# First batch: 1/Z folded into the summing matrix, the first tile divided at its store

## The chip, the cores and the metric

The kernel runs on one core of a Trainium2 chip. Its engines are TensorE (PE; its weight loads are listed apart as PEld), VectorE (DVE), ScalarE (ACT), GpSimd (POOL) and SyncE (SP, which issues the transfers); each works through its own queue in order, and they wait for one another by semaphores. The metric is the device time of one execution in microseconds. Before the change it is 1436.37 us, the median of 3 runs (1436.26 to 1436.56).

## The reference, cut to what matters

`x` is 4 x 12480 x 128, `inducing` 32 x 128, the feed-forward weights are 128 x 2048 and 2048 x 128. Inputs are float32 or, for the weights, doubles that the kernel turns into float32.

```python
def mab(q, kv):
    s = scale * (q @ kv.transpose(0, 2, 1))
    s = s - s.max(-1, keepdims=True)
    a = np.exp(s)
    a /= a.sum(-1, keepdims=True) + 1e-09
    return a @ kv
h = mab(I, x)                 # 32 inducing rows over 12480 rows, for each of 4 batches
x = mab(x, h)                 # each row over the 32 rows of h
h = x @ w_in
g = np.maximum(0.01 * h, h)
out = g @ w_out
```

## The kernel before, in words

**Tiles.** Each batch of 12480 rows is cut in six groups of 2048 rows and a rest of 192. A *tile* is 512 rows; tile 0 and tile 1 are the first two of batch 0. For a tile the kernel never forms `mab(x, h)`: with A the transposed softmax weights of its 512 rows (32 x 512, written four times, one copy for each 32 partitions), the first layer is `(h @ w_in)^T`-weights times A. The first-layer weights in that form are `hwhi` and `hwlo`, a high and a low part, made from h by `weights_product` and `split_weights`. A has a high and a low part too, and each first-layer block `f` (16 of 128 columns) is three products: hi·hi, lo·hi and hi·lo (`first_products`, line L1171). Four blocks are worked on side by side, each on 32 of the array's rows. The result goes through a ReLU on ScalarE (`ghi`, L1140) and leaves a low part (`glo`) that VectorE (L1144) or GpSimd (L1114 and L1116) makes; the second layer is three products again with `w_hi` and `w_lo` (L1202, a *triple* below). The linear part of the leaky ReLU goes by `w12` = 0.01·w_in·w_out (`setup_w12`, L349 to L357; `linear_part`, L1214).

**The start.** `first_batch` streams batch 0 in, and for each group forms scores against the inducing rows, a running maximum and sum, exponentials, and the weighted sum of rows `hacc`. When the last group is in, `sums` gives 1/Z as a column `rz`, `normalise` scales `hacc` by it on ScalarE (L674) and multiplies with the constant matrix `e128`, whose columns sum over the four positions at which a row of h lies (L680); a copy gives `hT` (L684). Beside it run: the conversion of the weights from doubles (`from_double`: `cv_a` on ScalarE, `cv_b`, `cv_a` and `cv_t` on VectorE, the last sum on GpSimd), the turning of w_in (`turn_w_in`, L318, copied at L324 or L326), the split of w_out (`split_w_out`, `w_hi` on ScalarE, `w_lo` on GpSimd), and `keep_going` (L337), products that nobody reads.

**The first two tiles.** Tiles 0 and 1 take a short way, `quick`: scores of the tile's 512 rows straight against `hT` (four products, L1029), maximum and subtraction on VectorE (L1036, L1040), exponential on ScalarE (L1044), sum, +1e-9, reciprocal and scaling on VectorE (L1047 to L1050), then 16 products with the identity that turn the weights and write them four times (L1058), and the copy into A, high part on ScalarE (L1064), low part on VectorE (L1067). Every other tile takes `second`, `softmax` and `stack`, the same in parts that run beside the feed-forward.

**The order.** All of it is emitted under a manual schedule: what stands later in a queue stays later. In the start the order is written by hand: `ROUNDS` and `DRAIN` say which side lane (`t` turning, `l` conversions, `s` split, `k` unread products, `d` turning with a VectorE copy) steps at which point of `first_batch`; then a tuple of lanes (L1312) orders the two `quick`s and the making of the first-layer weights; then the loop over `rounds` emits first-layer blocks of tiles 0 and 1 in turns of four, and after each second-layer triple the steps of `others(u)`, with `u` the count of triples. `first_round` emits the twelve first-layer products of four blocks. From tile 2 on a planner with modelled engine times sets the order. Eight PSUM banks are handed out in turn from small groups (`turns`); a bank is written again only when its reader is done. `store` (L1224 on) turns a finished tile on VectorE into `osb` and stores it by four transfers.

Of the kernel before, what the change touches and what calls it, by code (L numbers as in the profile page):

```python
# [19 lines left out]
def induced_attention_then_leaky_ffn(  # L20
# [24 lines left out]
    P = 128  # L45
# [33 lines left out]
    ]  # L79
    DRAIN = ["", "", "ll", "lldkk", "", ""]  # L80

# [87 lines left out]
    def new(engine, at=0.0):  # L169
        if quads[0]:  # L170
            yield engine, at
# [8 lines left out]
    def gen_ps(name):  # L180
        return bank("gen")
# [151 lines left out]

    def keep_going():
        while True:
            pt = gen_ps("keep_ps")
            nc.tensor.matmul(pt[:, : 2 * P], ident, w_in_sb[:, : 2 * P], start=True, stop=True)  # L337
            done(pt)
            yield

    def setup_w12():
        for c in range(NF // 4):
            while c >= len(ready):
                yield
            if c == len(ready) - 1:
                yield from idle(4)
# [322 lines left out]
    def normalise(b, hacc, rz):  # L669

        same = e128.rearrange("p j m -> p (j m)")
        yield from new(ACT, clock[DVE])
        hs = sb.tile([P, C], F32, tag="hs", name="hs", bufs=1)
# [18 lines left out]
    def first_batch():  # L692
# [98 lines left out]
        hacc = added(0, order[n - 2], hacc, al, hp)  # L791
        scale = sums(0)
        yield next(bg)
# [229 lines left out]
    def quick(t):  # L1023
# [13 lines left out]
        if not qys:  # L1037
            qys.append(sb.tile([P, QUICK, 4, M], F32, tag="both", name="qy", bufs=2))
        y = qys[0][:, t]
# [6 lines left out]
        sm = sb.tile([P, 4], F32, tag="sm", name="qsm")  # L1046
        nc.vector.tensor_reduce(out=sm, in_=y, op=ALU.add, axis=AX.X)  # L1047
        nc.vector.tensor_scalar_add(sm, sm, 1e-9)
        nc.vector.reciprocal(sm, sm)
        nc.vector.tensor_tensor(  # L1050
            out=y, in0=y, in1=sm.unsqueeze(2).broadcast_to([P, 4, M]), op=ALU.mult
        )
        yield
# [8 lines left out]
        yield  # L1062
        A4[t] = a4 = sb.tile([P, 2, TOK], F32R, tag="A4", name="A4", bufs=A4_BUFS)
# [7 lines left out]
        done(pa, at)  # L1071
        yield


    tiles = []
# [148 lines left out]
    def store(t, total, summed, at=0.0):  # L1224
# [9 lines left out]
        at = spent(DVE, BLOCKS, at)  # L1234
        if summed:
            parts_used[0] -= 1
        else:
            done(total, at)
# [58 lines left out]
    with tc.manual_schedule():  # L1297
        setup()
        late = [chain(setup_w_in(), setup_w_out())]
        turning, splits, twelve = [turn_w_in()], [parts_of_w_out()], [setup_w12()]  # L1300
        lanes = {"t": turning, "l": late, "s": splits, "k": [keep_going()]}
        for todo in first_batch():
# [6 lines left out]
        weights = [expand_weights(0)]  # L1309
        one, two, keep = [quick(0)], [quick(1)], lanes["k"]  # L1310
        for lane in (
            one, weights, two, one, weights, one, weights, one, keep, one, two, late, one, two,  # L1312
        ):
            step(lane)
# [5 lines left out]

        first_round(*rounds[0])
        timing[0] = True
        stacks[0] = stacks[0][QUICK:]
# [442 lines left out]
```

## Time and profile before

| | us |
|---|---|
| median of 3 runs | 1436.37 (1436.26 to 1436.56) |
| span of the profiled execution | 1434.7 |
| TensorE busy in it | 1418.0 |
| VectorE, ScalarE, GpSimd busy | 1070.6, 1066.0, 1178.9 |

The profiled execution is known by its span, from the first instruction to the last; the median of the timed runs lies 1.7 us above it. The rows below are of five kinds. The page is a summary of the whole span. The table by stretches gives the busy time of each engine between two moments, with the granted clock of TensorE as a share of its full rate. The timeline lists instructions in order of time, equal ones merged, with the idle time of the engine ahead of them in brackets and the instruction that ended it. The chain of waits is followed back from the last instruction, at each step to what released it. Times are from the start of the span. A matmul record's end is modelled and holds the array's latency, so that records overlap; the distance from one start to the next is what a product costs the queue. A float32 product that is no transpose shows as two records (passes).

### The profile page before, as it was taken

How to read it: one execution, taken by the hardware profiler on the slowest of the kernel's cores; microseconds unless marked ns; L12 is line 12 of the kernel's file. 1: busy time of each engine (PE TensorE's matmuls, PEld its weight loads, DVE VectorE, ACT ScalarE, POOL GpSimd, SP SyncE). 2: the span in 40 equal slices, each digit the busy share in tenths (PEclk: the TensorE clock that was granted, in tenths of full speed). 3: DMA queues.
4: the chain of work that ended last, by engine and by line, in shares of the span. 5: the costliest groups of instructions: out<-in, count | busy, mean ns of one | idle time of the engine just before them, and what ended most of it. 6: DMA issues, size and time to landing. Idle time of an engine off the chain costs nothing.

```text
span 1434.7 us, 60214 instructions
## 1 busy us (share of the span) xinstructions
PE 1418.0 (99%) x25207; PEld 1301.2 (91%) x25207; DVE 1070.6 (75%) x1913; ACT 1066.0 (74%) x1956; POOL 1178.9 (82%) x1237
## 2 busy tenths in 40 slices
PE   8999999999999999999999999999999999999998
PEld 6679899998889899998899999999989999999997
DVE  6777787776777787877777777877787876777664
ACT  6567777777777777777777787777777877778775
POOL 2369999899999888899999998885557588969996
PEclk9999999999999999999999999999999999999999
DMA  8055556433454553464445445534222333233231
GB/s 297 13 115 101 107 109 123 97 82 86 97 99 89 116 94 56 75 146 107 99 91 95 88 84 111 114 87 110 57 61 59 64 63 66 45 64 69 56 67 23
DMA packets 400703, 128.49 MB, mean 90 GB/s; under 512 B 373136, under 2 KB 375600, under 8 KB 400432
## 3 DMA queue, kind: packets, MB, share of 16 engines
q1 hardware_dynamic: 399328, 124.50, 41.7%
q8 instruction: 198, 3.24, 1.0%
q14 instruction: 73, 0.60, 0.1%
q10 hardware_dynamic: 1104, 0.15, 0.1%
HBM read 48.94 MB, written 25.56 MB: 52 GB/s over the span
## 4 chain that ended last, share of the span: by engine, by line
PE 94%; DVE 2%; ACT 1%; DMA 1%; issue 1%; POOL 1%; SPq 1%; DVEq 0%; ACTq 0%; POOLq 0%
PE bank L1171 87%; PE bank L398 3%; PE bank L578 2%; PE bank L1202 1%; DVE glo L1144 1%; PE bank L725 1%; DMA xr<-in_x_dram 1%; ACT ghi L1140 0%; DMA out_dram<-osb 0%; PE bank L820 0%; SPq L1012 0%; ACT xT L731 0%; POOL glo L1447 0%; PE bank L1058 0%; SPq L703 0%
## 5 line engine op out<-in xcount | busy, mean ns | idle before, releaser
L1171 PE MATMUL bank<-glo,w_hi 32*128 32x512 f32 (+1 forms) x6080 | 1165.1, 375 | 0.0
L1171 PE MATMUL bank<-ghi,w_hi 32*128 32x512 f32 (+1 forms) x6080 | 1164.7, 375 | 0.2
L1171 PE MATMUL bank<-ghi,w_lo 32*128 32x512 f32 (+1 forms) x6080 | 1164.8, 374 | 0.0
L1171 PE MATMUL bank<-A,hwhi 32*128 32x512 f32 (+1 forms) x3394 | 993.6, 373 | 0.8 <-DVE glo L1144 0.4
L1144 DVE SCALAR_TENSOR_TENSOR glo<-bank,ghi 128x512 fp32r<-128x512 f32 (+1 forms) x1047 | 687.2, 681 | 254.1 <-ACT ghi L1140 241.4
L1171 PEld LDWEIGHTS bank<-ghi,w_hi 32*128 32x128 f32 x6080 | 805.1, 184 | 16.5 <-issue 2.7
L1171 PEld LDWEIGHTS bank<-ghi,w_lo 32*128 32x128 f32 x6080 | 807.0, 184 | 12.4 <-issue 2.0
L1171 PEld LDWEIGHTS bank<-glo,w_hi 32*128 32x128 f32 x6080 | 806.8, 184 | 11.8 <-issue 1.0
L1140 ACT ACTIVATE ghi<-bank 128x512 fp32r<-128x512 f32 (+1 forms) x1047 | 608.0, 597 | 151.3 <-PE bank L1171 128.4
L1447 POOL TENSOR_TENSOR glo<-g,ghi 128x512 fp32r<-128x512 f32 (+1 forms) x513 | 656.0, 1279 | 41.1
L1171 PE MATMUL bank<-A,hwlo 32*128 32x512 f32 (+1 forms) x1697 | 586.2, 370 | 0.0
L1171 PEld LDWEIGHTS bank<-A,hwhi 32*128 32x128 f32 x3394 | 564.9, 184 | 16.6 <-DVE glo L1144 2.4
L1140 ACT ACTIVATE g<-bank 128x512 f32<-128x512 f32 (+1 forms) x521 | 311.2, 598 | 146.7 <-PE bank L1171 87.5
L1445 POOL CAST ghi<-g 128x512 fp32r<-128x512 f32 (+1 forms) x513 | 312.9, 610 | 106.5 <-ACT g L1140 80.0
L1171 PEld LDWEIGHTS bank<-A,hwlo 32*128 32x128 f32 x1697 | 299.9, 184 | 2.6 <-issue 0.2
L1481 DVE TENSOR_TENSOR part<-bank,part 128x512 f32<-128x512 f32 (+1 forms) x190 | 130.0, 685 | 60.7 <-PE bank L1171 38.3
L1492 POOL TENSOR_TENSOR part<-part 128x512 f32<-128x512 f32 (+1 forms) x95 | 121.4, 1277 | 22.5 <-DVE part L1481 22.1
L1474 ACT COPY part<-bank 128x512 f32<-128x512 f32 (+1 forms) x190 | 110.7, 584 | 12.4 <-PE bank L1171 10.5
L1229 DVE STREAM_TRANSPOSE osb<-part 128x512 f32<-128x512 f32 (+1 forms) x95 | 66.6, 701 | 6.6 <-POOL part L1492 4.9
L534 DVE STREAM_TRANSPOSE xT<-xc 128x512 f32<-128x512 f32 x72 | 46.5, 684 | 0.0
L455 ACT ACTIVATE e<-e,nm 128x512 f32<-128x512 f32 (+1 forms) x28 | 18.7, 667 | 22.9 <-DVE least L443 22.7
L936 POOL TENSOR_TENSOR y<-y,mx 128x512 f32<-128x512 f32 (+1 forms) x24 | 24.4, 1018 | 9.6 <-DVE mx L932 8.3
(135 smaller groups left out, 646.1 us busy)
## 6 DMA issues: line engine op xcount, KB each, us to landing
A<-both SPq DMA_DIRECT2D x376, 128.0 KB, 2.4
xr<-in_x_dram SPq DMA_DIRECT2D x96, 256.0 KB, 4.3
out_dram<-osb SPq DMA_DIRECT2D x382, 64.0 KB, 2.2
xc<-in_x_dram SPq DMA_DIRECT2D x288, 64.0 KB, 2.9
raw<-in_moe_w_in_dram SPq DMA_DIRECT2D x4, 512.0 KB, 6.6
raw<-in_moe_w_out_dram SPq DMA_DIRECT2D x4, 512.0 KB, 7.4
A<-both SPq DMA_DIRECT2D x48, 16.0 KB, 1.8
out_dram<-osb SPq DMA_DIRECT2D x48, 8.0 KB, 1.8
```

What stands on the lines that cost most here:

```text
L398: nc.tensor.matmul(dst, lhsT, rhs, start=True, stop=True)
L534: nc.vector.transpose(t[:, j, :], blk.rearrange("p n c -> p (n c)"))
L578: nc.tensor.matmul(hp[32 * k : 32 * k + 32, :C], ay[:rows_, 4 * q + k, :], xb[:rows_, k, :], start=(q == 0), stop=(4 * q + 4 >= K), tile_p ...
L1140: nc.scalar.activation(ghi, ph, AF.Relu)
L1144: nc.vector.scalar_tensor_tensor(out=glo, in0=ph, scalar=0.0, in1=ghi, op0=ALU.max, op1=ALU.subtract,)
L1171: nc.tensor.matmul(dst, w[32 * r : 32 * r + 32], woven(x[32 * r : 32 * r + 32]), start=start, stop=stop, tile_position=(32 * r, 0),)
L1229: nc.vector.transpose(osb[:, :n], total[:, :n])
L1445: nc.gpsimd.tensor_copy(ghi[:, :n], g[:, :n])
L1447: nc.gpsimd.tensor_tensor(out=glo[:, :n], in0=g[:, :n], in1=ghi[:, :n].bitcast(F32), op=ALU.subtract)
L1474: nc.scalar.copy(put, got)
L1481: nc.vector.tensor_tensor(out=put, in0=got, in1=put, op=ALU.add)
L1492: nc.gpsimd.tensor_tensor(out=total[:, :n], in0=total[:, :n], in1=part[:, :n], op=ALU.add)
```

## The change

Four edits, all in the start of batch 0 and in the store of tile 0.

- `first_batch` makes `scale`, the constant `e128` times `rz`, on ScalarE as soon as `rz` is there; `normalise` for batch 0 multiplies `hacc` itself with it.
- `quick(0)` doesn't divide by the sum. Its exponential is written four times (two ScalarE instructions of 128 x 256), so that four transposes of 128 x 128 give the four copies of the turned weights. The sums, their reciprocals, and 16 small products that turn the reciprocals into one factor per partition and 32 columns (`over`) come at `u == 7`. `store` multiplies `osb` of tile 0 by `over` on GpSimd. (The layers behind are homogeneous, so that a positive factor per row may come at the end.)
- `keep_going` is gone.
- The hand-written orders move: the last turning of w_in goes from the first rounds into `DRAIN` (`"t"` in place of `"kk"` and the empty steps), `late` goes ahead of `one`, the second tile's `quick` behind the first one's, and the first step of `w12` behind the first `first_round`.

The diff, cut:

```diff
-    DRAIN = ["", "", "ll", "lldkk", "", ""]
+    DRAIN = ["", "", "ll", "lld", "", "t"]
...
+        if not b:
+            ph = aux_ps("hT_ps")
+            nc.tensor.matmul(ph[:, :P], hacc, rz, start=True, stop=True)
+            yield
+            hT = sb.tile([P, P], F32, tag="hT", name="hT")
+            nc.scalar.copy(hT, ph[:, :P])
...
-        scale = sums(0)
+        rz = sums(0)
+        scale = sb.tile([P, P], F32, tag="hs", name="scale", bufs=1)
+        nc.scalar.mul(scale, e128.rearrange("p j m -> p (j m)"), rz)
...
-        nc.scalar.activation(y, y, AF.Exp, scale=SCALE)
+        if t:
+            nc.scalar.activation(y, y, AF.Exp, scale=SCALE)
+        else:
+            four = qys[0][:, : 4 * P].rearrange("p (c r m) -> p c r m", r=4, m=M)
+            for c in (0, 2):
+                nc.scalar.activation(
+                    four[:, c : c + 2], y[:, c : c + 2].unsqueeze(2).broadcast_to([P, 2, 4, M]),
+                    AF.Exp, scale=SCALE,
+                )
...
         for c in range(4):
+            if not t:
+                nc.tensor.transpose(
+                    pa[:, c * P : (c + 1) * P], qys[0][:, c * P : (c + 1) * P], ident
+                )
+                continue
             for r in range(4):
...
+        sm = total(four[:, :, 0])
+        pr = aux_ps("rows_ps")
+        rows_of_k = pr[:, : 4 * 4].rearrange("p (c a) -> p c a", a=4)
+        for a in range(4):
+            for r in range(4):
+                nc.tensor.matmul(
+                    rows_of_k[32 * r : 32 * r + 32, :, a], ident[:, 32 * a : 32 * a + 32], sm,
+                    start=True, stop=True, tile_position=(0, 32 * r),
+                )
+        over = sb.tile([P, 16], F32, tag="over", name="over", bufs=1)
+        nc.scalar.copy(over, pr[:, :16])
...
+            nc.gpsimd.tensor_tensor(
+                out=ov, in0=ov, in1=overs[t].unsqueeze(2).broadcast_to([P, 16, 32]), op=ALU.mult
+            )
...
-            one, weights, two, one, weights, one, weights, one, keep, one, two, late, one, two,
-        ):
+        for lane in (late, one, weights, one, weights, weights, one, two, one, two, two):
             step(lane)
...
         first_round(*rounds[0])
+        step(twelve)
...
+                if u == 7:
+                    step(one)
```

**Place 1.** TensorE from the third turning of w_in (L318) to the turned weights of the two quick tiles, before: L337 are the unread products, L680 the summing product, L1029 the scores, L820 the first-layer weights, L1058 the 16 products that turn tile 0's weights.

```order
L318 MATMUL bank_65<-ident,w_in_sb 128x128 x4
L337 MATMUL bank_66<-w_in_sb,ident 128x256
L337 MATMUL bank_64<-w_in_sb,ident 128x256
L680 MATMUL bank_70<-e_74,hs 128x128
L1029 MATMUL bank_71<-hT,xT 128x32 x4
L820 MATMUL bank_70<-w_in_sb,hT 32x512 x4
L1029 MATMUL bank_65<-hT,xT 128x32 x4
L1058 MATMUL bank_67<-ident,qy 32x128 x16
L337 MATMUL bank_66<-w_in_sb,ident 128x256
```

The same stretch now; L667 is the summing product, L1035 the scores, L826 the first-layer weights, L1078 the transposes.

```order
L318 MATMUL bank_65<-ident,w_in_sb 128x128 x4
L667 MATMUL bank_70<-scale,hacc 128x128
L318 MATMUL bank_66<-ident,w_in_sb 128x128 x4
L1035 MATMUL bank_71<-hT,xT 128x32 x4
L826 MATMUL bank_70<-w_in_sb,hT 32x512 x4
L1078 MATMUL bank_67<-ident,qy 128x128 x4
L1035 MATMUL bank_64<-hT,xT 128x32 x4
```

The unread products are gone, the fourth turning of w_in stands behind the summing product, and the second tile's scores stand behind the transposes of the first.

**Place 2.** TensorE in the second turn of four blocks, before: triples of tile 1 (bank3_67; here the tiles are printed with their numbers) and the next first products of tile 1 (A4_752).

```order
L1202 MATMUL bank3_67<-ghi_779,w_hi_77 128x512
L1202 MATMUL bank3_67<-ghi_779,w_lo_78 128x512
L1202 MATMUL bank3_67<-glo_780,w_hi_77 128x512
L1202 MATMUL bank3_67<-ghi_783,w_hi_77 128x512
L1202 MATMUL bank3_67<-ghi_783,w_lo_78 128x512
L1202 MATMUL bank3_67<-glo_784,w_hi_77 128x512
L1171 MATMUL bank5_69<-A4_752,hwhi_659 128x512
L1171 MATMUL bank1_65<-A4_752,hwhi_659 128x512
```

The same now; L1107 are the 16 small products, L342 a step of w12.

```order
L1247 MATMUL bank3_67<-ghi_771,w_hi_77 128x512
L1247 MATMUL bank3_67<-ghi_771,w_lo_78 128x512
L1247 MATMUL bank3_67<-glo_772,w_hi_77 128x512
L1107 MATMUL bank7_71<-qsm_837,ident_72 32x4 x16
L1247 MATMUL bank3_67<-ghi_775,w_hi_77 128x512
L1247 MATMUL bank3_67<-ghi_775,w_lo_78 128x512
L1247 MATMUL bank3_67<-glo_776,w_hi_77 128x512
L342 MATMUL bank6_70<-wraw_619,winT_569 128x128 x4
L1216 MATMUL bank1_65<-A4_744,hwhi_662 128x512
L1216 MATMUL bank2_66<-A4_744,hwhi_662 128x512
```

The small products stand between two triples, ahead of the next first products. VectorE at the same place, before: the last low part of tile 0's second four blocks, a conversion (L216), maximum and subtraction of a softmax (L932, L936), a conversion (L220), and low parts of tile 1's second four blocks.

```order
L1144 SCALAR_TENSOR_TENSOR glo_829<-bank0_64,ghi_828 128x512
L216 TENSOR_SCALAR cv_b_837<-raw_308 128x512
L932 TENSOR_REDUCE mx_846<-y_800 128x16
L936 TENSOR_TENSOR y_800<-y_800,mx_846 128x512
L220 SCALAR_TENSOR_TENSOR cv_a_836<-cv_a_836,cv_b_837 128x512
L1144 SCALAR_TENSOR_TENSOR glo_873<-bank5_69,ghi_872 128x512
L1144 SCALAR_TENSOR_TENSOR glo_883<-bank2_66,ghi_882 128x512
```

The same now; L1063 to L1065 make the sums' reciprocals, and the small products read them.

```order
L1189 SCALAR_TENSOR_TENSOR glo_815<-bank0_64,ghi_814 128x512
L216 TENSOR_SCALAR cv_b_823<-raw_308 128x512
L938 TENSOR_REDUCE mx_827<-y_786 128x16
L942 TENSOR_TENSOR y_786<-y_786,mx_827 128x512
L220 SCALAR_TENSOR_TENSOR cv_a_822<-cv_a_822,cv_b_823 128x512
L1063 TENSOR_REDUCE qsm_837<-qy_658 128x4
L1064 TENSOR_SCALAR qsm_837<-qsm_837 128x4
L1065 RECIPROCAL qsm_837<-qsm_837 128x4
L348 SCALAR_TENSOR_TENSOR w12_79<-bank6_70,w12_79 128x128
L1189 SCALAR_TENSOR_TENSOR glo_881<-bank1_65,ghi_880 128x512
```

The three short steps stand behind the conversions and the softmax's subtraction, and a step of w12 (L348) stands ahead of the low parts.

**Place 3.** GpSimd around the first store, before: w_lo's last part, a low part, a softmax's subtraction (L936) and the low part of A (L996).

```order
L288 TENSOR_TENSOR w_lo<-wraw,w_hi 128x512
L1114 CAST ghi<-g 128x512
L1116 TENSOR_TENSOR glo<-g,ghi 128x512
L936 TENSOR_TENSOR y<-y,mx 128x512
L996 TENSOR_TENSOR both<-aT,both 128x512
L1445 CAST ghi<-g 128x512
```

The same now.

```order
L288 TENSOR_TENSOR w_lo<-wraw,w_hi 128x512
L1159 CAST ghi<-g 128x512
L1161 TENSOR_TENSOR glo<-g,ghi 128x512
L1282 TENSOR_TENSOR osb<-osb,over 128x512
L942 TENSOR_TENSOR y<-y,mx 128x512
L1002 TENSOR_TENSOR both<-aT,both 128x512
L1496 CAST ghi<-g 128x512
```

The multiply of osb stands ahead of the subtraction. Behind these places the order of every engine is the same as before, in operations and tiles (bank and buffer numbers apart), to the end.

## Rows read from the trace of the kernel before

**Rows 1.** The profile's page, its first line.

```profile
span 1434.7 us, 60214 instructions
```

**Rows 2.** Busy time by stretch: us; busy us (instructions) per engine, granted clock, DMA share, GB/s.

```profile
36.00:56.00 20.00, 18.16 (x227) 11.76 (x228) 14.65 (x34) 10.41 (x22) 5.70 (x5) 1.00 0.04 7
...
56.00:64.00 8.00, 8.00 (x55) 6.45 (x54) 6.17 (x11) 5.38 (x11) 3.57 (x4) 1.00 0.00 0
...
64.00:92.00 28.00, 26.59 (x168) 17.71 (x170) 23.45 (x43) 14.05 (x27) 15.02 (x15) 1.00 0.38 70
...
160.00:1400.00 1240.00, 1238.54 (x22872) 1152.59 (x22872) 934.28 (x1617) 944.29 (x1723) 1061.31 (x1113) 1.00 0.43 87
```

**Rows 3.** Timeline, 38 to 48 us: start, duration (us), engine, line, operation, [idle before].

```profile
38.49 0.35 DVE L597 SCALAR_TENSOR_TENSOR hacc<-hacc,al,bank 128x128 f32<-128x128 f32 x1 [0.34 <-PE bank L578]
...
40.45 1.08 PE L1029 MATMUL bank<-hT,xT 128*128 128x32 f32 x8 [0.35 <-ACT hT L684]
...
44.79 0.58 ACT L1064 CAST A<-bank 128x512 fp32r<-128x512 f32 x1 [1.60 <-PE bank L1058]
...
46.67 2.07 ACT L1140 ACTIVATE ghi<-bank 128x512 fp32r<-128x512 f32 x4 [1.08 <-PE bank L1171]
...
47.30 2.48 DVE L1144 SCALAR_TENSOR_TENSOR glo<-bank,ghi 128x512 fp32r<-128x512 f32 x4
```

**Rows 4.** Timeline, 53 to 62 us, TensorE and VectorE.

```profile
53.28 0.66 PE L318 MATMUL bank<-ident,w_in_sb 128*128 128x128 f32 x4 [0.56 <-DVE glo L1144]
...
54.86 0.49 PE L1171 MATMUL bank<-A,hwhi 32*128 32x512 f32 x4
...
55.40 0.38 PE L1171 MATMUL bank<-A,hwhi 32*128 32x512 f32 x4
...
56.47 1.05 PE L349 MATMUL bank<-wraw,winT 128*128 128x128 f32 x8
...
56.93 1.89 DVE L1144 SCALAR_TENSOR_TENSOR glo<-bank,ghi 128x512 fp32r<-128x512 f32 x3 [1.21 <-ACT ghi L1140]
...
60.47 0.68 DVE L220 SCALAR_TENSOR_TENSOR cv_a<-cv_a,cv_b 128x512 int32<-128x512 int32 x1
...
61.73 0.69 DVE L1144 SCALAR_TENSOR_TENSOR glo<-bank,ghi 128x512 fp32r<-128x512 f32 x1 [0.58 <-ACT ghi L1140]
```

**Rows 5.** Timeline: small operations of the first batch.

```profile
34.24 0.39 PE L482 MATMUL bank<-rd,e 128*128 128x4 f32 x2 [0.21 <-DVE rd L424]
...
42.55 0.29 DVE L1047 TENSOR_REDUCE qsm<-qy 128x4 f32<-128x128 f32 x1 [0.38 <-ACT qy L1044]
...
48.46 1.08 PE L1058 MATMUL bank<-ident,qy 128*32 128x128 f32 x32
```

**Rows 6.** Stretches of TensorE alone: us, busy us (instructions), granted clock, DMA share, GB/s.

```profile
11.00:12.00 1.00, 0.26 (x2) 0.93 1.04 410
...
1430.00:1432.00 2.00, 0.00 (x0) 0.95 0.25 44
```

**Rows 7.** Chain of waits: start, duration (us), engine, tile, line, instructions.

```profile
11.74 3.62 PE bank L725 x16
...
17.09 1.90 PE bank L725 x16
...
91.41 27.90 PE bank L1171 x491
```

**Rows 8.** Timeline, 91 to 98 us: first store, GpSimd, ScalarE, one TensorE product.

```profile
91.47 1.43 DVE L1233 STREAM_TRANSPOSE osb<-bank 128x256 f32<-128x256 f32 x4
...
91.73 1.05 POOL L936 TENSOR_TENSOR y<-y,mx 128x512 f32<-128x512 f32 x1
...
94.89 1.28 POOL L1447 TENSOR_TENSOR glo<-g,ghi 128x512 fp32r<-128x512 f32 x1
...
96.46 0.63 ACT L1140 ACTIVATE g<-bank 128x512 f32<-128x512 f32 x1
...
97.45 0.37 PE L1171 MATMUL bank<-A,hwhi 32*128 32x512 f32 x1
```

More of the change, by code (lines that the diff above doesn't have):

```diff
@@ L332, in turn_w_in @@
             yield
[L334 to L339, printed above, removed]
     def setup_w12():
@@ L344, in setup_w12 @@
                 yield
-            if c == len(ready) - 1:
+            if c and c == len(ready) - 1:
                 yield from idle(4)
@@ L671, in normalise @@
         same = e128.rearrange("p j m -> p (j m)")
+        if not b:
[4 more added lines that the diff above has]
+            nc.scalar.copy(hT, ph[:, :P])
+            done(ph)
+            hw[b] = [hT, None, None, False]
+            finishing[0] = 1
+            yield
+            return
         yield from new(ACT, clock[DVE])
@@ L1037, in quick @@
         if not qys:
-            qys.append(sb.tile([P, QUICK, 4, M], F32, tag="both", name="qy", bufs=2))
-        y = qys[0][:, t]
+            qys.append(sb.tile([P, 4 * P + 2 * P], F32, tag="both", name="qy", bufs=2))
+        y = qys[0][:, 4 * P + t * P : 4 * P + (t + 1) * P].rearrange("p (c m) -> p c m", m=M)
         nc.vector.tensor_tensor(
@@ L1043, in quick, with total @@
         done(sp)
-        nc.scalar.activation(y, y, AF.Exp, scale=SCALE)
-        yield
[L1046 to L1053, printed above, removed]
+        if t:
[7 more added lines that the diff above has]
+                )
+        yield
+        def total(y):
+            sm = sb.tile([P, 4], F32, tag="sm", name="qsm")
+            nc.vector.tensor_reduce(out=sm, in_=y, op=ALU.add, axis=AX.X)
+            nc.vector.tensor_scalar_add(sm, sm, 1e-9)
+            nc.vector.reciprocal(sm, sm)
+            return sm
+        if t:
+            sm = total(y)
+            nc.vector.tensor_tensor(
+                out=y, in0=y, in1=sm.unsqueeze(2).broadcast_to([P, 4, M]), op=ALU.mult
+            )
+            yield
         pa = bank("out")
@@ L1061, in quick @@
                 )
-        yield
+        if t:
+            yield
         A4[t] = a4 = sb.tile([P, 2, TOK], F32R, tag="A4", name="A4", bufs=A4_BUFS)
@@ L1072, in quick @@
         yield
+        if t:
+            return
+        sm = total(four[:, :, 0])
+        spent(DVE, 640.0)
+        pr = aux_ps("rows_ps")
[8 more added lines that the diff above has]
+        nc.scalar.copy(over, pr[:, :16])
+        at = spent(ACT, 200.0, on_array("c", 60.0))
+        done(pr, at)
+        overs[t] = over
+        yield
+    overs = {}
     tiles = []
@@ L1234, in store @@
         at = spent(DVE, BLOCKS, at)
+        if t in overs:
+            ov = osb.rearrange("p (k c) -> p k c", c=32)
+            nc.gpsimd.tensor_tensor(
+                out=ov, in0=ov, in1=overs[t].unsqueeze(2).broadcast_to([P, 16, 32]), op=ALU.mult
+            )
         if summed:
@@ L1300, in induced_attention_then_leaky_ffn @@
         turning, splits, twelve = [turn_w_in()], [parts_of_w_out()], [setup_w12()]
-        lanes = {"t": turning, "l": late, "s": splits, "k": [keep_going()]}
+        lanes = {"t": turning, "l": late, "s": splits}
         for todo in first_batch():
@@ L1309, in induced_attention_then_leaky_ffn @@
         weights = [expand_weights(0)]
-        one, two, keep = [quick(0)], [quick(1)], lanes["k"]
-        for lane in (
-            one, weights, two, one, weights, one, weights, one, keep, one, two, late, one, two,
-        ):
+        one, two = [quick(0)], [quick(1)]
+        for lane in (late, one, weights, one, weights, weights, one, two, one, two, two):
             step(lane)
```

## The prediction, before the run

> **What bounds the kernel now.** I read the table by stretches first. From 160 to 1400 us TensorE is busy 1238.54 of 1240.00 us; in 64 to 92 us it is busy 26.59 of 28.00 [rows 2], and the chain of waits runs on TensorE alone for 27.90 us from 91.41 us [rows 7]. So past some 92 us the order of TensorE's work is the time: a microsecond that its queue is late there stays to the end, and one that it is early is kept. The order of the changed kernel is the same as before, engine by engine, after that point, but for one GpSimd multiply at the first store. The change is therefore decided between 38 and 92 us, and there I read the timeline row by row [rows 3, 4].
>
> In that stretch two engines take turns as the bound. Up to 47 us it is one serial chain (h, scores, softmax, A, first layer, ReLU) [rows 3]. From 57 us on VectorE has no room: the three low parts that start at 56.93, the conversions of w_out and a softmax follow each other to 61.15, then the next low part starts at 61.73 [rows 4]. What VectorE does behind that (conversions, from which GpSimd makes w_lo, for which TensorE waits) sets TensorE's pace up to 92 us. So the moment at which this row of 61.73 us starts is my measure of the whole start.
>
> **The change part by part.**
>
> *1/Z in the summing matrix, no unread products.* h's sum is ready on VectorE at 38.49 + 0.35 = 38.84; the scaling on ScalarE, the unread products, the summing product and a copy follow, and the first scores start at 40.45 [rows 3]. Now the product reads the sum itself, and the scaled matrix is made on ScalarE before the sum is there: the product goes at about 38.9, the scores at about 39.65, 0.8 earlier. The turning of the last chunk of w_in fills the wait for h; before, it stood at 53.28 [rows 4].
>
> *Undivided exponentials, written four times.* Between the exponential and the cast of A at 44.79 [rows 3] stand four VectorE steps, the first at 42.55, and 32 passes (1.08) [rows 5]. The steps go away, the passes become four transposes. It costs a second exponential and one cast ahead on ScalarE, some 0.4 and 0.5. By these steps the cast of A is at about 43.05, 1.7 earlier. But this does not carry through. The second tile's scores now come behind the transposes (until about 43.9), its maximum and subtraction behind A's low part (until about 44.9), and the fourth first-layer product writes the bank in which those scores lay; so the ReLUs go at 45.6, not at 46.67. The second tile's division still stands ahead of the first low part on VectorE: about 46.25 instead of 47.30 [rows 3]. I take **1.05 earlier**; the ends are 0.8 (nothing but the first item) and 1.7 (the cast's gain carries through).
>
> *The moved turning.* Without the turning and its wait at 53.28, the first products of blocks 4 to 7 of tile 0 are held by the low part of tile 1's fourth block alone: their third group, at 55.40 before [rows 4], starts at about 54.15, 1.25 earlier.
>
> *The four steps, put back later.* The sums of the first tile, their reciprocals and their turning (16 small products) still have to be made. In the new order VectorE has them behind the three low parts, a conversion, a maximum, a subtraction and another conversion; TensorE has the 16 products ahead of block 3 of tile 1. That is a new wait, with the whole TensorE queue behind it. TensorE is there three triples after the third group: 54.15 + 0.31 + 3 x 0.65 = 56.4. VectorE needs from that third group to the end of the second conversion what it needed before, 60.47 + 0.68 - 55.40 = 5.75 [rows 4], and then a reduction of 0.29 as in [rows 5] and two short steps, 0.7 together: 54.15 + 5.75 + 0.7 + 0.05 = 60.65. **TensorE waits 4.2 us.**
>
> Nothing covers this. Behind it TensorE has the 16 products, block 3, a w12 product and the next first products, whose ReLU and low part VectorE waits for. The trace has no product of this shape. Its bounds are 0.4 (two passes with 4 columns, 0.39, if the other 30 passes cost next to nothing) and 1.08 (32 passes with 128 columns) [rows 5]; I take 0.9, nearer to the second, which has the same number of passes and of weight loads. So the low part that was at 61.73 starts at 60.65 + 0.9 + 0.85 (block 3 and two changes of tiling) + 0.8 (the w12 product: 56.47 to its successor) + 0.92 (twelve first products, 54.86 to 55.78) + 0.65 (one ReLU and its signals) = 64.8: **3.05 later**. One w12 step of VectorE is now ahead of it, which gives back 0.2: **2.85**. What stood ahead of 61.73 before was ScalarE's exponential, so none of the start's gain is left there.
>
> *The clock.* The granted clock was at the upper level (2.4 GHz, shown as 1.00) in all of 36 to 92 us [rows 2]. It fell to the lower one in the stretch 11 to 12 us, after TensorE had been busy 0.26 us of one, and in 1430 to 1432, a stretch without a product [rows 6]. Sixteen transposes took 3.62 us there and 1.90 at the upper level: 1.7 lost [rows 7]. A wait of 4.2 us is longer than that second stretch, so I expect a fall in it. The low level begins partly inside the wait, where it costs nothing: I take **1.2**, with ends 0 (no fall) and 2.4 (a second such stretch in part).
>
> The Trainium skill speaks against the change here. "TensorE: Matmul & The Clock Gate", Part 1 (the HAM clock gate), says that "the default state is throttled, and activity releases the throttle"; the change takes out the unread products, which were activity alone, and adds a wait. By that page the clock would fall in the new wait, and the sum would be 1441.2 with it and 1440.0 without; the two falls in the trace agree.
>
> *The scaling at the store.* GpSimd gets a 128x512 multiply ahead of the subtraction that started at 91.73; it waits for the first two of the four pieces of osb, until about 92.2, and takes about 1.05, as the subtraction of that shape did [rows 8]. So GpSimd is 1.5 late, less 0.15 of idle time: 1.35. Its next low part, 94.89 + 1.28, frees the buffer (g has two) that the ScalarE row of 96.46 writes (slack 0.3), and that row frees the bank that TensorE writes at 97.45 (slack 0.35) [rows 8]. TensorE is held for about **0.75**; ends 0 and 1.35. SyncE's store waits 1.1 longer, and behind it stands an A load for a tile that begins more than 10 us later: nothing.
>
> **Sum.** 2.85 + 1.2 + 0.75 = 4.8 on a span of 1434.7 [rows 1] gives 1439.5; the median of the runs, 1436.37, lies 1.7 above the span, and I keep that: **1441.2**.
>
> **The rivals.**
> - *The clock holds.* The same wait, without the fall: 1441.2 - 1.2 = 1440.0. For it: in 36 to 92 us it never fell. Against: no wait there came near 4 us.
> - *Later waits absorb it.* TensorE is idle 1.4 us in 64 to 92 us [rows 2], waiting for VectorE and GpSimd. If these did not move with the delay, because their own chain had room, 1.4 would come back, and with the bank of the store hidden 0.75 more: 1441.2 - 2.2 = 1439.0, and with the clock held too 1437.8. Against it: VectorE waits for the very products that are late.
> - *Not slower: the small products' operand is in time.* It decides at about 56.4 us: if VectorE's reciprocals were done by then, TensorE would not wait, the 1.25 of the third group would stay, and a GpSimd that is earlier by as much would hide the store. Time: 1436.4 - 1.25 = 1435.1. Against it: VectorE would have to be 4 us ahead of its rows. That the change doesn't shorten what it names is no case: it does, by 1.7 at the cast.
> - *Two low stretches and the full store delay:* 1441.2 + 1.2 + 0.6 = 1443.0.
>
> **How the numbers follow.** The forecast has 0.60, the clock that holds 0.15, absorption 0.13, in time 0.06, the worst 0.06. 0.2% (about what a measurement of this kernel can tell from no change) is 2.87 us, so slower begins at 1439.24. The first, second and last case lie above (0.81, of which I take off 0.04 for small products at their lower bound with the clock held); absorption and in time are within; faster by that much needs a gain of which I see half at most. Range: below, 1438.6 takes in the clock that holds with small products at 0.4 and half of absorption; above, 1443.0 the worst.
>
> **What would show it.** In the new trace: the summing product near 38.9 and the cast of A near 43; first low part near 46.2; then a TensorE wait of about 4 us, released by VectorE's reciprocal, ahead of 32 short passes near 60.6; a granted clock below 1.00 between 56 and 66 us; the fifth block's low part near 65, not 61.7; the unbroken TensorE chain beginning near 95 to 96 us. A wait under 2 us at the small products would make the forecast wrong, a clock of 1.00 throughout would make its third term wrong.

## The result, and the profile after

The changed kernel took **1443.21 us** (median of 5 executions, 1441.31 to 1446.37) against 1436.26 us of the kernel before (5 executions beside them): a ratio of 1.0052, 95% interval 1.0041 to 1.0064, or 6.95 us more. The forecast was 1441.2 us in 1438.6 to 1443.0: the sign was right, the time 2.0 us above it and 0.2 us above the range. The executions lie farther apart than those of before (5.06 us against 1.27), and the profiled one is the longest, 1446.37 us. So its trace may hold more than the median execution does.

The page's first line, and TensorE's clock by stretch (us; busy us with instructions, granted clock, DMA share, GB/s):

```profile
span 1444.6 us, 60212 instructions
```

```profile
44.00:45.00 1.00, 0.38 (x4) 0.80 0.07 10
45.00:51.00 6.00, 6.00 (x52) 0.50 0.08 11
56.00:64.00 8.00, 4.14 (x54) 1.00 0.00 0
64.00:65.00 1.00, 1.00 (x8) 1.00 0.00 0
65.00:68.00 3.00, 3.00 (x19) 0.51 0.00 0
```

Before, these stretches were all at 1.00 [rows 2]. Now the clock is at its lower level (1.2 GHz, shown as 0.50) twice: from 44 to 51 us, where the forecast had no fall, and from 65 to 68 us (the two low stretches, below). And TensorE is busy 4.14 of 8 us in 56 to 64, where it was busy throughout. The timeline of the same places (start, duration, engine, line, operation, idle time and what ended it):

```profile
38.71 0.46 PE L667 MATMUL bank<-scale,hacc 128*128 128x128 f32 x2
...
42.73 0.58 ACT L1090 CAST A<-bank 128x512 fp32r<-128x512 f32 x1
...
44.62 0.79 PE L1216 MATMUL bank<-A,hwhi 32*128 32x512 f32 x1 [0.69 <-DVE qy L1046]
...
46.51 2.48 DVE L1189 SCALAR_TENSOR_TENSOR glo<-bank,ghi 128x512 fp32r<-128x512 f32 x4 [0.54 <-ACT ghi L1185]
...
49.47 1.94 PE L1083 MATMUL bank<-ident,qy 128*32 128x128 f32 x32
...
57.08 0.59 PE L1216 MATMUL bank<-A,hwhi 32*128 32x512 f32 x4
...
63.19 0.18 DVE L1065 RECIPROCAL qsm<-qsm 128x4 f32<-128x4 f32 x1
63.42 0.43 PE L1107 MATMUL bank<-qsm,ident 128*32 128x4 f32 x32 [3.62 <-DVE qsm L1065]
...
68.26 0.69 DVE L1189 SCALAR_TENSOR_TENSOR glo<-bank,ghi 128x512 fp32r<-128x512 f32 x1 [1.97 <-ACT ghi L1185]
```

The start is what the change promised: the cast of A at 42.73 was at 44.79 [rows 3]. (0.27 of this gain is not the change's: h's last sum starts at 38.22 in this trace, at 38.49 in before.) Then the 32 passes at 49.47 take 1.94 instead of 1.08 [rows 5], because they lie in the first low stretch, and the third group of tile 0's first products of blocks 4 to 7 (57.08) is later than before (55.40 [rows 4]), not earlier. Then the forecast wait: 3.62 us of TensorE, ended by VectorE's reciprocal. The fifth block's low part, my measure of the start, is at 68.26 instead of 61.73.

The chain of waits of after shows what comes on top (start, duration, engine, tile, line):

```profile
91.85 0.99 PE bank L391 x8
...
98.88 1.05 POOL osb L1282
99.93 1.01 POOL y L942
100.94 1.26 POOL both L1002
...
102.83 1.29 POOL glo L1498
...
104.15 0.60 ACT g L1185
...
161.16 16.69 PE bank L1216 x304
...
704.42 1.06 PE bank L826 x8
```

and of before, the three rows that answer to its first and its last two:

```profile
85.29 1.00 PE bank L398 x8
...
153.54 16.69 PE bank L1171 x304
...
694.50 1.07 PE bank L820 x8
```

The new kernel is 6.56 us late at the first pair, 7.62 at the second, 9.92 at the third. So 6.56 us come from the start, 1.06 from the first store (before, this chain ran on TensorE alone [rows 7]; now it runs through five GpSimd steps and ScalarE's buffer g), and 2.3 from somewhere between 161 and 704 us. Most of that last piece is a wait of VectorE for a store, here in after and in before (after has a second one, of 1.29 us, that ends at 625.80):

```profile
641.16 0.71 DVE L1274 STREAM_TRANSPOSE osb<-part 128x512 f32<-128x512 f32 x1 [2.81 <-DMA out_dram<-osb]
```

```profile
631.24 0.71 DVE L1229 STREAM_TRANSPOSE osb<-part 128x512 f32<-128x512 f32 x1 [1.22 <-DMA out_dram<-osb]
```

Before itself loses some 0.8 us there against a trace without such a wait (the kernel before without its unread products, below).

### The profile page after: what moved, and what is told of

It reads as the page before. It is cut to its first block, busy times and chain, and to the rows that moved or that the text cites. A ratio compares the mean times of both kernels' runs of the same rounds, so it can differ in the third digit from the quotient of the medians.

```text
span 1444.6 us, 60212 instructions
## 1 busy us (share of the span) xinstructions
PE 1423.3 (99%) x25205; PEld 1300.1 (90%) x25205; DVE 1070.3 (74%) x1912; ACT 1066.7 (74%) x1958; POOL 1179.5 (82%) x1238
## 4 chain that ended last, share of the span: by engine, by line
PE 91%; DVE 3%; DMA 2%; SPq 2%; ACT 1%; issue 1%; POOL 1%; DVEq 0%; ACTq 0%; POOLq 0%
PE bank L1216 85%; PE bank L391 3%; PE bank L571 1%; PE bank L1247 1%; SPq L1300 1%; DMA xr<-in_x_dram 1%; DVE glo L1189 1%; DMA raw<-in_moe_w_in_dram 0%; DMA out_dram<-osb 0%; ACT ghi L1185 0%; ACT g L1185 0%; PE bank L342 0%; PE bank L729 0%; PE bank L826 0%; DVE sm L956 0%
## 5 line engine op out<-in xcount | busy, mean ns | idle before, releaser
L1002 POOL TENSOR_TENSOR both<-aT,both 128x512 fp32r<-128x512 f32 x24 | 31.6, 1317 | 0.8 <-ACT both L995 0.7
```

Source lines behind the costliest of these rows:

```text
L1002: (eng or nc.gpsimd).tensor_tensor(out=alo[sl], in0=aT.pop((b, g))[: 32 * J, :], in1=ahi[sl].bitcast(F32), op=ALU.subtract,)
```

## The experiments

My theory after the result: the wait at the small products is the core; the clock falls at two places, not at one; the multiply costs 1.1 us; the late store is not the change's. All runs are compared with the kernel before on the same chip (medians there: 1436.21, 1435.67 and 1435.05 us), so between chips the ratios are to be compared, not the times. The line numbers of a changed copy can be a few off those of after.

**The changed kernel again**, no edit.

> The changed kernel once more, unaltered, for a second profile. Theory (two low stretches of the clock, a wait of 3.6 us at the small products, the multiply at the store): the profile again shows a TensorE wait of 3 to 4.5 us released by VectorE's reciprocal near 60 us, and the granted clock below 1.00 behind it; the runs lie between 1441 and 1444 us, and the late stores at 636 to 641 us, which held VectorE 2.81 us in the first profile, are not there or below 1.5 us. Rival (the late stores belong to the change, and cost 2.3 us in every run): VectorE waits over 2 us for a store near 640 us again.

Measured: 1442.56 us (1441.10 to 1444.24), ratio 1.0044 (1.0032 to 1.0057). Its profile is of the fastest execution, span 1439.3. TensorE by stretch, and three rows of the timeline:

```profile
44.00:52.00 8.00, 7.30 (x80) 1.00 0.08 12
...
56.00:60.00 4.00, 0.99 (x5) 1.00 0.00 0
60.00:64.00 4.00, 3.40 (x43) 0.62 0.00 0
64.00:68.00 4.00, 4.00 (x29) 0.96 0.00 0
```

```profile
54.26 0.59 PE L1216 MATMUL bank<-A,hwhi 32*128 32x512 f32 x4
...
60.60 0.43 PE L1107 MATMUL bank<-qsm,ident 128*32 128x4 f32 x32 [3.62 <-DVE qsm L1065]
...
65.92 0.69 DVE L1189 SCALAR_TENSOR_TENSOR glo<-bank,ghi 128x512 fp32r<-128x512 f32 x1 [1.27 <-ACT ghi L1185]
```

The first row of its chain of waits that answers to 91.85 in after and 85.29 in before:

```profile
89.48 1.00 PE bank L391 x8
```

The same program, without the first low stretch, though TensorE waits ahead of the same product as before the fall in after:

```profile
44.95 0.48 PE L1216 MATMUL bank<-A,hwhi 32*128 32x512 f32 x1 [0.70 <-DVE qy L1046]
```

The third group is where it was forecast (54.15), and so are the small products (60.65). The chain's row is 4.19 us late instead of 6.56. No wait for a store near 640 us is in this trace at all. So neither the late store nor the first low stretch is in every execution of this program; the late store is in before too.

**Unread products put back** at one place.

```diff
-        for lane in (late, one, weights, one, weights, weights, one, two, one, two, two):
+        for lane in (late, one, weights, one, weights, weights, one, two, keep, one, two, two):
```

(`keep` issues two products of 128x256 that nobody reads.)

> The changed kernel with two unread products of 128x256 behind the second tile's scores, where TensorE was idle 0.69 us. Theory (the first low stretch, 44.6 to 51.4 us, comes from the missing products): the granted clock is 1.00 in 44 to 52 us, the third group of first products of blocks 4 to 7 of tile 0 starts near 54.2 instead of 57.1, the wait at the small products stays at 3.5 to 4.5 us, and the time falls by 2.9 to about 1440.3. Rival (the stretch comes from the new order of waits, whatever runs in 43.5 to 44.6): the low stretch stays and the time is 1443.2, or a little more for the products' own 0.9 us.

Measured: 1441.57 us, ratio 1.0036 (1.0023 to 1.0050): 1.0 less than the run above, where 2.9 was expected; the intervals overlap. TensorE by stretch:

```profile
44.00:52.00 8.00, 8.00 (x84) 1.00 0.08 12
...
59.00:60.00 1.00, 0.00 (x0) 0.88 0.00 0
60.00:64.00 4.00, 3.44 (x42) 0.50 0.00 0
```

```profile
60.56 0.61 PE L1115 MATMUL bank<-qsm,ident 128*32 128x4 f32 x32 [3.62 <-DVE qsm L1073]
```

No fall at 44 us, as expected, but this is one profile, and the run above had none either. The fall at the wait is longer here, and it begins inside the wait: the clock is 0.88 in 59 to 60 us, and the small products come at 60.56. From them to the next low part it took 6.20 us (60.56 to 66.76), in the run above 5.32. The chain's row is at 90.33, 5.04 us late.

**The sums early.**

```diff
         sm = total(four[:, :, 0])
-        spent(DVE, 640.0)
+        yield
...
-        for lane in (late, one, weights, one, weights, weights, one, two, one, two, two):
+        for lane in (late, one, weights, one, weights, weights, one, two, one, two, two, one):
```

> The changed kernel with VectorE's three short steps (reduction, addition, reciprocal) directly behind the second tile's division, ahead of the first low part; the 16 small products stay where they are. Theory (the wait at the small products and the fall of the clock in it are the main part): no wait there, no low stretch in 60 to 70 us, the fifth block's low part near 63.4 instead of 68.3, since VectorE's conversions then bound it, and 1443.2 - 4.8 = 1438.4 us. Rival (the waits behind absorb it: GpSimd and VectorE set the pace up to 92 us anyway): the wait goes, but no more than 1.5 us comes back, 1441.7 us or more.

Measured: **1436.54 us**, ratio 1.0005 (0.9996 to 1.0014), 11 executions. From its timeline:

```profile
54.92 0.59 PE L1216 MATMUL bank<-A,hwhi 32*128 32x512 f32 x4
...
57.58 0.44 PE L1107 MATMUL bank<-qsm,ident 128*32 128x4 f32 x32
...
61.32 0.69 DVE L1189 SCALAR_TENSOR_TENSOR glo<-bank,ghi 128x512 fp32r<-128x512 f32 x1 [0.47 <-ACT ghi L1185]
```

No wait, clock 1.00 in all of 36 to 92 us, and the low part at 61.32, where before had it at 61.73. Moving 0.63 us of VectorE's work gives back nearly all that the change cost. The rival, absorption, has fallen. More came back than the 4.8 us expected: I had counted from a third group at 57.08, and this profile has no first low stretch either. In its chain of waits the kernel is 0.39 us early where before has 85.29, and 0.70 late where before has 153.54: the multiply at the store, 1.09 us, is what is left of the loss. Three of its 11 executions (1437.95 to 1438.02 us) ran at a mean granted clock of 0.997 or 0.998, the others at 0.999 or 1.0.

**No multiply at the store.** Tile 0's output stays unscaled.

```diff
-        if t in overs:
+        if False:
```

> The changed kernel without GpSimd's multiply at the first tile's store (that tile stays unscaled; all else runs). Theory (the multiply holds TensorE through GpSimd's queue and ScalarE's g buffer): the chain of waits no longer goes through GpSimd at 98 to 104 us, and the time falls by 1.05 to about 1442.1. Rival (GpSimd's delay is hidden behind other work): the same time within 0.3 us.

Measured: 1442.38 us, ratio 1.0041 (1.0029 to 1.0054). The median says nothing; its trace does. The chain of waits:

```profile
90.73 1.00 PE bank L391 x8
...
94.07 1.29 PE bank L1259 x6
...
96.85 27.91 PE bank L1216 x491
```

From the first of these rows to the last TensorE alone is on the chain, as in before from 85.29 to 91.41 [rows 7], and it is 5.44 us late at both ends: nothing is lost here. With the multiply on GpSimd, 1.06 to 1.09 us were lost in each trace. This execution had both low stretches (44 to 52 us at a mean of 0.79) and a wait of 2.47 us for a store at 638 us, which hid the gain in its time.

**The wait filled.** Eight unread products ahead of the small ones, into unused columns of their bank.

```diff
+        for _ in range(8):
+            nc.tensor.matmul(pr[:, 2 * P :], ident, w_in_sb[:, : 2 * P], start=True, stop=True)
         rows_of_k = pr[:, : 4 * 4].rearrange("p (c a) -> p c a", a=4)
```

> The changed kernel with eight unread products of 128x256 in the wait ahead of the 16 small products, into unused columns of their bank; the wait itself stays. Theory (the fall of the clock in the wait costs 1.2 us by itself): granted clock 1.00 from 56 to 70 us, from the small products to the next low part 4.1 us instead of 4.8 to 5.3, and 1442.8 - 1.2 = 1441.6 us. Rival (the low stretch lies beside work of VectorE and ScalarE and costs nothing): 1442.8 us.

Measured: **1440.01 us**, ratio 1.0032 (1.0021 to 1.0044). From its timeline:

```profile
54.08 0.59 PE L1218 MATMUL bank<-A,hwhi 32*128 32x512 f32 x4
...
56.64 3.62 PE L1105 MATMUL bank<-w_in_sb,ident 128*128 128x256 f32 x16
60.42 0.44 PE L1109 MATMUL bank<-qsm,ident 128*32 128x4 f32 x32 [0.16 <-DVE qsm L1065]
...
64.17 0.69 DVE L1191 SCALAR_TENSOR_TENSOR glo<-bank,ghi 128x512 fp32r<-128x512 f32 x1 [1.25 <-ACT ghi L1187]
```

and from its chain of waits, the rows that answer to 85.29 and 153.54 in before:

```profile
87.69 1.00 PE bank L391 x8
...
157.01 16.69 PE bank L1218 x304
```

The wait is as long as ever, but TensorE works in it, and the clock is 1.00 throughout. From the small products to the low part it takes 3.75 us; in the four profiles with the wait unfilled it takes 4.84 (the first one of after), 5.32, 5.35 (without the multiply) and 6.20. So up to the low part the fall at the wait costs 1.1 to 2.4 us. Of its 6 executions, four at a mean clock of 1.0 took 1438.98 to 1440.51 us; two at 0.997 and 0.995 took 1441.41 and 1443.24; where the clock fell in these, no profile shows.

**Both fillings.** The last edit and the second together.

```diff
-        for lane in (late, one, weights, one, weights, weights, one, two, one, two, two):
+        for lane in (late, one, weights, one, weights, weights, one, two, keep, one, two, two):
...
+        for _ in range(8):
+            nc.tensor.matmul(pr[:, 2 * P :], ident, w_in_sb[:, : 2 * P], start=True, stop=True)
```

> The changed kernel with both fillings: eight unread products in the wait for the sums and two behind the second tile's scores; every wait of the changed kernel stays. Theory (all that the change costs beyond the wait, the small products and the store's multiply is low clock, and it falls at two places, near 44 and in the wait): every execution at a mean granted clock of 0.999 or more, all between 1438.9 and 1440.6 us, median 1439.7. Rival (the slower executions of the run with the wait filled, 1441.4 and 1443.2 at 0.997 and 0.995, have another cause than missing products at 44 us): some executions again at 0.997 or below and above 1441 us.

Measured: 1440.15 us, ratio 1.0032 (1.0020 to 1.0044). Five of six executions are at 0.999 or 1.0 and 1438.42 to 1440.23 us; one is at 0.998 and 1441.51. These are nearly the times that the theory expects, but on a chip where before is 0.6 faster: against before it is 5.10 us, with the wait alone filled 4.34, and the ratios are the same. So the two products brought nothing that the medians show. One slower execution is left.

**All three edits** (sums early, two products back, multiply on VectorE).

```diff
-        for lane in (late, one, weights, one, weights, weights, one, two, one, two, two):
+        for lane in (late, one, weights, one, weights, weights, one, two, keep, one, two, two, one):
...
-        spent(DVE, 640.0)
+        yield
...
-            nc.gpsimd.tensor_tensor(
+            nc.vector.tensor_tensor(
                 out=ov, in0=ov, in1=overs[t].unsqueeze(2).broadcast_to([P, 16, 32]), op=ALU.mult
```

> The changed kernel with three edits at once: the three short VectorE steps early (as in the run with early sums, 1436.54), two unread products of 128x256 behind the second tile's scores, and the multiply at the first store on VectorE instead of GpSimd. Theory (the multiply costs 1.1 us on GpSimd's queue, the missing products cost a low stretch in some executions): no wait at the small products, no GpSimd step in the chain of waits at 90 to 98 us, granted clock 1.00 in 40 to 56 us, 1436.54 - 1.1 = 1435.4 us, the runs closer together than 2 us. Rival (the multiply only changes queues: VectorE's next low part waits for it as GpSimd's did): 1436.2 us or more.

Measured: 1434.65 us, ratio 0.9991 (0.9982 to 1.0000), 1.0 below the kernel before, with an interval that reaches to no change. The multiply takes 1.05 us on VectorE as well, but in the chain of waits GpSimd's five steps are gone and TensorE's unbroken run begins at 93.42 us; with the sums early and the multiply on GpSimd it begins at 97.85. What the move is worth is less: the chain is 0.65 us early where before has 85.29 and 0.05 late where before has 153.54, so the multiply costs 0.70 here and 1.09 on GpSimd. The move gives 0.4 us, not the 1.1 expected.

**Sums early and the multiply on VectorE, without the products.**

```diff
-        spent(DVE, 640.0)
+        yield
...
-        for lane in (late, one, weights, one, weights, weights, one, two, one, two, two):
+        for lane in (late, one, weights, one, weights, weights, one, two, one, two, two, one):
...
-            nc.gpsimd.tensor_tensor(
+            nc.vector.tensor_tensor(
```

> The changed kernel with the three short VectorE steps early and the multiply at the first store on VectorE; no unread products. Theory (the multiply's place is worth 1.0 us, since on GpSimd it delays two low parts, and the products are worth nothing but the slower executions): 1436.5 - 1.0 = 1435.5 us against a before of 1436.2, that is 0.6 below the before of the same chip, with two or three executions in ten 1.5 us higher at a lower clock. Rival (the gain of the run with all three edits came from its unread products): no better than the before of the same chip.

Measured: 1435.65 us against 1435.05, ratio 1.0003 (0.9994 to 1.0012). Expected was 0.6 below. The rival's value (no better than before) is what came, though the interval holds both. Its profile caught the first low stretch:

```profile
44.00:52.00 8.00, 8.00 (x73) 0.79 0.07 10
```

Nothing waits for the sums in this kernel, so the first fall needs no such wait.

**The kernel before without its unread products.**

```diff
-    DRAIN = ["", "", "ll", "lldkk", "", ""]
+    DRAIN = ["", "", "ll", "lld", "", ""]
...
-            one, weights, two, one, weights, one, weights, one, keep, one, two, late, one, two,
+            one, weights, two, one, weights, one, weights, one, one, two, late, one, two,
```

> The kernel before without its unread products, and nothing else. Theory (they keep the clock up between 39 and 52 us): some executions show a mean granted clock of 0.998 or less and take 1.5 us more, so the median rises to about 1437.0 and the highest run to 1438. Rival (they do nothing there): median 1436.2 within 0.3 us, no run above 1437.5.

Measured: 1435.77 us against 1435.67, ratio 1.0000 (0.9992 to 1.0009), 11 executions, the highest 1437.02. The median rose by 0.10, where my theory had 0.8; the interval, up to 1.3 us, does not exclude that. Five of the 11 executions are at a mean clock of 0.998, one of 28 of before. Its profile shows no fall, though TensorE is busy for less of this stretch than in any other:

```profile
44.00:52.00 8.00, 6.57 (x80) 1.00 0.07 10
```

**Two parts alone**: the kernel before with 1/Z in the summing matrix and the fourth turning in the wait for h; the two unread products that stood there go, a step of w12 moves as in the change, and the divided exponentials stay.

```diff
-    DRAIN = ["", "", "ll", "lldkk", "", ""]
+    DRAIN = ["", "", "ll", "lld", "", "t"]
...
-        scale = sums(0)
+        rz = sums(0)
+        scale = sb.tile([P, P], F32, tag="hs", name="scale", bufs=1)
+        nc.scalar.mul(scale, e128.rearrange("p j m -> p (j m)"), rz)
...
         first_round(*rounds[0])
+        step(twelve)
```

> The kernel before with two parts of the change alone: 1/Z in the summing matrix and the fourth turning of w_in in the wait for h (and so without the two unread products that stood there; the one behind A stays); the divided exponentials and their 32 passes stay as before. Theory (these two parts gain what was forecast for the start, 0.8 to 1.25 us, and nothing gives it back): the first low part about 0.8 us and the third group of tile 0's blocks 4 to 7 about 1.2 us earlier than before, 1435.2 us. Rival (VectorE's conversions set the pace behind it): the third group is earlier, the fifth block's low part is not, 1436.2 us.

Measured: **1433.89 us**, ratio 0.9988 (0.9980 to 0.9997), the kernel that beats both. From its timeline:

```profile
38.96 0.46 PE L674 MATMUL bank<-scale,hacc 128*128 128x128 f32 x2
39.25 0.60 PE L318 MATMUL bank<-ident,w_in_sb 128*128 128x128 f32 x4
...
54.51 0.59 PE L1184 MATMUL bank<-A,hwhi 32*128 32x512 f32 x4
...
60.76 0.69 DVE L1157 SCALAR_TENSOR_TENSOR glo<-bank,ghi 128x512 fp32r<-128x512 f32 x1 [0.38 <-ACT ghi L1153]
```

The third group is 0.89 and the low part 0.97 earlier than before, and 0.99 of it is left at 153.54 us of before; the median shows 1.78, and what the rest is stays open. Some 0.4 of the 0.99 is also in the profile of the kernel before without its unread products. The same without the one product that it kept:

```diff
-            one, weights, two, one, weights, one, weights, one, keep, one, two, late, one, two,
+            one, weights, two, one, weights, one, weights, one, one, two, late, one, two,
```

> The kernel before with 1/Z in the summing matrix and the turning in the wait for h, and without any unread product. Theory (at this place the products do nothing for the time, as the kernel before without them showed): 1.8 us below the before of the same chip, within 0.4 us of the run that kept one product, no low stretch in 40 to 56 us. Rival (with the shorter chain the clock falls in some executions, as in the changed kernel): the median within 1 us of the kernel before, with executions at 0.998 and below.

Measured: 1433.88 us, ratio 0.9989 (0.9981 to 0.9998): 1.2 below the before of its chip instead of 1.8, in ratio the same as the run that kept one product. All 11 executions are at 0.999 or 1.0, and in its profile the clock is 1.00 in all of 36 to 92 us.

## Why the prediction was off, step by step

| step | forecast | profile after | with the clock held (wait filled) |
|---|---|---|---|
| cast of A | 43.05 | 42.73 | |
| third group of tile 0's blocks 4 to 7 | 54.15 | 57.08 | 54.08 |
| small products | 60.65 | 63.42 | 60.42 |
| wait ahead of them | 4.2 | 3.62 | 3.62 of filling + 0.16 |
| their cost to the next triple | 0.9 | 0.37 | 0.37 |
| the low part that was at 61.73 | 64.8 + clock | 68.26 | 64.17 |
| the multiply at the store | 0.75 | 1.06 | 1.07 |
| delay at the chain's first row (before: 85.29) | 2.85 + clock | 6.56 | 2.40 |
| clock, at that row | 1.2 | 4.2 | 0 |

**Right.** The chain from h to A, that the cast's gain would not carry through, the order behind it, VectorE's list of work ahead of the reciprocals, the wait and what is queued behind it, the path of the multiply through GpSimd and the buffer g. The forecast without its clock term was 3.6 us; in the profile with the wait filled the chain is 2.40 late ahead of the store and 3.47 behind it (157.01 against 153.54). The medians differ by more, 4.34 with the wait filled and 5.10 with both fillings; two of the six executions of the first had a lower mean clock, and no trace accounts for the rest. That the sum without the clock comes so near is in part luck, as the next two errors partly cancel.

**Too large or too small.** The 16 small products cost 0.37 instead of 0.9, just under the lower end (0.4); I had chosen by the number of passes and weight loads, and with the same number the columns (4 against 128) made the difference. The multiply cost 1.06 instead of 0.75 (the terms as written, 1.35 less 0.3 and 0.35, make 0.70): against the start's delay ScalarE's row is 1.13 late (104.15 against 96.46) and TensorE 1.06, so of the slack of 0.35 that I subtracted at the bank 0.07 was there. The wait was 3.62 instead of 4.2 since TensorE came to it later, at 56.98 instead of 56.4 in the second profile; VectorE was done when forecast, so this costs nothing.

**Wrong: the third term, the clock.** I allowed one fall of the clock, in the wait, with part of it inside the wait: 1.2 us. At the first row of the chain of waits the four profiles with the wait unfilled are 4.19, 5.04, 5.44 and 6.56 us late, against 2.40 with the wait filled. So the low clock cost 1.8 to 4.2 us there: 1.8 and 2.6 with one fall, 3.0 and 4.2 with two.

The first error is where the fall lies. In the traces it begins between 0.8 us ahead of the wait's end and 1.6 us behind it. In the profile with the products put back it begins inside, some 0.8 us ahead (an estimate from the 0.88 in 59 to 60 us and the small products at 60.56). In the second profile of the changed kernel the clock is 0.97 in 60 to 61 us, with the small products at 60.60, and 0.50 from 61 to 64. In the first profile the fall comes at 65 us, 1.6 us after TensorE was busy again. So most of it lies on work.

The second error is a fall that I had only in a rival, the one at 1443.0 with a chance of 0.06: near 44 us, in three of the profiles (the first one of after, the one without the multiply, the one with the sums early and the multiply on VectorE). It made the third group and the small products 2.82 us later in the first profile of after than in the second (57.08 against 54.26, 63.42 against 60.60). In the first profile this is the larger part of the miss: its fall at the wait cost 1.1 up to the low part, about what I had allowed. I had costed "no unread products" at nothing since the clock was at 1.00 in all of 36 to 92 us before. That shows that it did not fall, not what held it.

The Trainium skill ("TensorE: Matmul & The Clock Gate", Part 1) says of the number of slow products at a kernel's start that "it's run-variable". The traces agree, and beyond a start: the same program fell at 44 us in one execution and not in another. By its rule that "activity releases the throttle" the filled wait should keep the clock up; it did, 1.00 from 56 to 70 us.

**What stays open.** What brings the first fall. It is in three of the six profiles of the changed order with no unread products ahead of 52 us, in none of the three with them, and in none of the four of the kernel before and its variants, with or without them. That fits the order and the products together, but these are few profiles, and the medians (1.0036 with the products back against 1.0044) don't tell them apart. The wait of some 0.7 us just ahead of it does not decide it alone: it is also in profiles without the fall (the second one of the changed kernel, the sums early, the kernel before without its products). And the wait for a store near 640 us (2.81, 2.47, 1.22 us, or none) varies from trace to trace; in the first profile it cost 2.3 us more than in before. No run tested its cause.

## What to carry to other kernels

Work that is put off must be put where its operands' engine is free, not only where its result is first needed: three VectorE steps of 0.63 us in all, left behind that engine's other work, cost some 6 us, and 13 us earlier in its list (46.45 instead of 59.85) they left the kernel level with the one before. Price each wait of TensorE twice, by its length and by the half-speed work behind it. Take a second profile before building on a fall of the clock, as one execution falls where another doesn't. When a change of several parts loses, run its parts alone: here two of them were worth 1.2 to 1.8 us by the medians, and about 1 us in the traces.

## What the runs showed of the hardware

- A fall of the granted clock need not begin in the idle stretch that it follows. In the first profile of the changed kernel TensorE waited until 63.42 us, was busy all of 64 to 65 us at 1.00, and stood at 0.51 in 65 to 68. With the products put back the clock was 0.88 in 59 to 60 us, while the wait lasted to 60.56.
- A long wait is not needed for a fall, and a short one is no sure sign of it. TensorE was busy 7.57 of 8 us in 36 to 44 us of the changed kernel in both profiles and then waited 0.69 and 0.70 us; the clock fell behind it in one execution and not in the other. The kernel before without its unread products was busy 6.57 of 8 us in 44 to 52 us, at 1.00.
- 32 passes of 4 columns took 0.43 us and held the next product by 0.37, where 32 of 128 columns take 1.08 [rows 5]. At the lower clock the same 32 passes of 4 columns took 0.61 (products put back).
- The 128x512 multiply with a broadcast factor took 1.05 us on GpSimd and 1.05 on VectorE. The latter ran beside work of GpSimd, whose next step (`both`) took 1.74 us there instead of 1.30 in before; VectorE's subtraction of the same shape with a broadcast operand took 0.69 in after (61.46 us), with GpSimd idle. So the price on VectorE is that of a place where both engines work; no run moved it to another.
